# A float32 first-unit attention for the second unit too: one head per step of the first MLP

## The chip, the cores and the metric

One core of one Trainium2 chip runs the whole program. The metric is the device time of one execution in microseconds (us). Engines are named as the profile names them: PE is TensorE's matmul stream and PEld its weight loads, DVE is VectorE, ACT is ScalarE, POOL is GpSimd, SP is SyncE, whose queue issues nearly all transfers of this kernel.

## What is computed

A decayed causal attention over 4 batches, 8 heads, 576 tokens and a head size of 64 feeds an MLP with a squared ReLU, and that feeds an MLP with a leaky ReLU. Both MLPs are 512 to 2048 to 512 wide, over 2304 tokens.

```python
scores = scale * np.matmul(q, k.transpose(0, 1, 3, 2))
cum = np.cumsum(np.log(np.clip(f, 0.0001, 1.0)), axis=-1)
decay = cum[:, :, :, None] - cum[:, :, None, :]
scores = np.where(causal, -1000000000.0, scores + decay)
attn = np.exp(scores - np.max(scores, axis=-1, keepdims=True))
attn = attn / (np.sum(attn, axis=-1, keepdims=True) + 1e-09)
x = np.matmul(attn, v)                       # then heads side by side: 2304 x 512
r = np.maximum(x @ w_in, 0.0)
x = (s * (r * r) + b) @ w_out                # first MLP
h = x @ w_in2
out = np.maximum(0.01 * h, h) @ w_out2       # second MLP
```

## The kernel before

The tokens are cut into eight units (`unit_list`, L32): units 0 to 3 are the first 256 tokens of batches 0 to 3, units 4 to 7 the tokens 256 to 575. A ninth unit collects the last 64 tokens of each batch. The first MLP runs unit by unit (the loop at L816), in NF = 16 steps of 128 hidden channels. A step does `mlp1_h` (12 matmuls of L680 into one PSUM bank), `mlp1_g` on ACT, and `mlp1_o` of the step before. In unit 0 the hidden values stay float32 and `mlp1_o` is four float32 matmuls, which the trace shows as eight records of L721. In the later units it is twelve float32r matmuls (L724).

The attention of a unit must be finished when its MLP starts, so it runs beside the MLP of the unit before. There are two ways of doing it.

**The first way** (`first_a`, `first_b`, `first_c`, L529 to L601) is used for unit 0 alone, ahead of any MLP. For each head `first_a` makes scores of two query tiles (128 and 256 keys) with float32 matmuls (L540), adds the decay with a float32r matmul (L541) and the mask with a bfloat16 one (L542). DVE takes the maximum (L543, L547), and ACT the exponential with its sum (L551). `first_b` has two small DVE instructions for the reciprocal (L564, L565), scales the rows on POOL (L569), transposes three 128x128 blocks on PE (L578) and copies them out of PSUM on ACT (L580). `first_c` multiplies with V in float32 (L589) and splits the result into a high and a low float32r part (L598 on ACT, L599 on DVE). The three parts of a head run in three successive rounds.

**The second way** works in slots, one tile of queries of a head per slot. For the units 1 to 3 a head is one slot, so each has eight. A slot splits K and Q into two float32r parts (`split_head`: POOL L244, L245, DVE L246, L247) and V into two float16 parts (`split_v`: DVE L265 to L278, POOL L274, L277, and a transposing DMA, L283). `st_score` makes scores with float32r matmuls (L308) and a mask (L317), adds the decay row and takes the minimum in one DVE instruction (L320), and takes the exponential on ACT (L336). `st_split` normalizes into two float16 parts (DVE L346, L347, L358, ACT L357) and transposes them by a DMA (L362). `st_av` multiplies with V (L379) and collects (ACT L398, L413, DVE L399, L414). Loads of Q and K (`qk_raw`, L212), of V (L215) and of decay rows (`cumk`, L229) go through SP's queue.

**Weights.** The first MLP's weights come as 32 blocks of 64-bit floats (512 KB each, L89 and L94). `float_w` turns one into float32 with one ACT (L102) and three DVE instructions (L103, L104, L106); `split_w` makes the two float32r parts of a block (ACT L111, POOL L112). Step i of unit 0 needs the blocks 2i and 2i+1. Before the first MLP ten blocks are floated, the rest in unit 0's loop (L832 to L836). The output blocks get their split in unit 1 (`split_late_to`). Pool `wp` has 33 buffers (L72); Q and K of unit 0, V, the identity and the decay rows lie in it too. The tag `tt` has four buffers, shared by scores, exponentials and the temporary of `float_w`.

**Order.** A list scheduler arranges the instructions of each engine by a priority, which is the order of the program less the offset of `ahead(n)`: slots have 150, weights -100 (they fill what is left), the first way 0. `slots_to(slot_target(u, i))` says how many slots are emitted by step i of unit u. In unit 0's loop that grows from 1 to 11: unit 1's eight heads and the first three of unit 2.

Of the kernel before, what the change touches and what calls it, by code (L numbers as in the profile page):

```python
# [18 lines left out]
NQ = 384  # L19
UN = 256  # L20
QT = [(0, 128), (128, 128), (256, 128), (384, 128), (512, 64)]
PSCALE = 2.0**14
# [17 lines left out]
def attention_moe_moe_kernel(  # L40
# [124 lines left out]

    heads = [(u, h) for u in range(1, NU - 1) for h in range(H)]

# [261 lines left out]
    def ahead(n):  # L429
        return tc.high_priority(offset=n)  # L430
# [5 lines left out]
    W_BACK = 3  # L436
    W_AHEAD = 1
    LEAD = 1
# [30 lines left out]
    nc.scalar.preload_act_table_set("natural_log_exp_and_others")  # L469
    for r in range(ND // 2):  # L470
# [12 lines left out]

    cl = wp.tile([P, 2 * DM], F32R, tag="w", name="cum_hl")
    for a in range(P // BH):
        nc.gpsimd.tensor_scalar(
            cl[a * BH : (a + 1) * BH, S : S + H],
            ident[a * BH : (a + 1) * BH, a * BH : a * BH + H],
            -INV,
            0.0,  # L490
            ALU.mult,
            ALU.add,
        )
# [12 lines left out]
    for e in range(2):  # L506
# [11 lines left out]
    nc.vector.tensor_tensor_scan(cum, f_sb, f_sb, 0.0, ALU.add, ALU.bypass)  # L518
    nc.scalar.copy(cl[:BH, :S], cum)
    nc.vector.tensor_tensor(  # L520
        out=cl[BH : 2 * BH, :S], in0=cum, in1=cl[:BH, :S].bitcast(F32), op=ALU.subtract
    )
# [4 lines left out]
    e_0, sm_0, pt_0 = {}, {}, {}  # L527
    xs[0] = xp.tile([P, 2, ND, UN], F32R, tag="x", name="x", bufs=2)
    def first_a(h):  # L529
        rows = slice(h % 2 * D, (h % 2 + 1) * D)  # L530
        qt = qk_0[h // 4][rows, h // 2 % 2]
        ps = ps_o.tile([P, 512], F32, tag=f"o{h % 2}", name="ps_s0")
        e = e_0[h] = ap.tile([P, S], F32, tag="tt", name="e_0", bufs=4)
        sm = sm_0[h] = ap.tile([P, 5 * NT0], F32, tag="sm_0", name="sm_0", bufs=3)
        neg = cl[rows, S + h : S + h + 1]
        at = 0
# [45 lines left out]
    def first_c(h):  # L582
        pt = pt_0.pop(h)
        av = ps_h.tile([P, 512], F32, tag="h", name="av_0")
        pr, own = h // 2, slice(h % 2 * D, (h % 2 + 1) * D)
        at = 0
        for k in range(NT0):
            n = un0 - k * P
            nc.tensor.matmul(  # L589
                av[:, k * P : un0],  # L590
                v_0[:, k, pr * P : (pr + 1) * P],
                pt[:, at : at + n],
                start=(k == 0),
                stop=(k == NT0 - 1),
            )
            at += n
        x = xs[0]
        nc.scalar.copy(x[own, 0, pr, :un0], av[own, :un0])  # L598
        nc.vector.tensor_tensor(  # L599
            out=x[own, 1, pr, :un0], in0=av[own, :un0], in1=x[own, 0, pr, :un0].bitcast(F32), op=ALU.subtract  # L600
        )  # L601

    for h in range(H + 2):
        with ahead(P_F):
            if h >= 2:
                first_c(h - 2)
            if 1 <= h <= H:
                first_b(h - 1)
            if h < H:
                first_a(h)  # L610
# [12 lines left out]
        if h == 7:  # L623
            load_cumk(1)

# [190 lines left out]
    for u in range(NU):  # L816
# [9 lines left out]
        for i in range(NF):  # L826
# [112 lines left out]
```

## Time and profile before

| | |
|---|---|
| time, median of 3 runs | 1087.61 us (1086.0 to 1089.47) |
| the profiled execution | 1090.52 us, of which the profile's span is 1088.7 us |
| PE busy over the span | 1013.7 us (93%) |
| DVE busy | 609.9 us (56%) |
| ACT busy | 525.9 us (48%) |
| POOL busy | 242.0 us (22%) |
| first unit's attention alone | 9.4 to about 48 us |
| first unit's MLP, beside unit 1's attention | about 50 to 142 us |
| second unit's MLP, beside unit 2's attention | 142 to 222 us |

A busy share is a mean over stages that have different limits, so the profile is read by stage. Matmul records overlap (one starts before the one ahead of it ends), so the pace of PE is read from start times, not from durations. DVE records overlap a little too.

### The profile page before, as it was taken

Reading aid. Unit: us, or ns where it says so; the run is one execution under the profiler, and the core shown is the slowest. Engines: PE = TensorE matmul, PEld = TensorE weight load, DVE = VectorE, ACT = ScalarE, POOL = GpSimd, SP = SyncE. Lnnn points to the kernel's source line nnn. Section 1 sums busy time; section 2 is a strip of 40 time slices with the busy share of each in tenths; the row PEclk is TensorE's granted clock in tenths of the full one; section 3 lists DMA queues with packets and bytes.
Section 4 is the critical chain, followed back from the end, with each engine's and each line's share of the span. In section 5 each row is a group of like instructions: output and inputs, shape, how many; then the busy total and the mean of one; then the engine's idle time right before and its main releaser. Section 6 shows DMA issues by size and latency. Waiting matters only on the chain.

```text
span 1088.7 us, 18609 instructions
## 1 busy us (share of the span) xinstructions
PE 1013.7 (93%) x6728; PEld 885.8 (81%) x6728; DVE 609.9 (56%) x1522; ACT 525.9 (48%) x1283; POOL 242.0 (22%) x346
## 2 busy tenths in 40 slices
PE   7887889899899899888999999999999999999998
PEld 4676688798788788888899999777888888888887
DVE  6889988676687787777754158984311311211121
ACT  4566677565566565666664356653222222222122
POOL 5344455522122322222200014542000000000000
PEclk9999899999999999999899999999999999999999
DMA  8488465568788978889842065540200100010010
GB/s 278 159 190 242 127 150 115 132 158 165 149 191 187 199 169 190 198 175 204 190 89 78 1 208 180 174 155 0 78 1 1 59 1 1 1 39 1 1 39 20
DMA packets 188333, 127.74 MB, mean 117 GB/s; under 512 B 137488, under 2 KB 163600, under 8 KB 188240
## 3 DMA queue, kind: packets, MB, share of 16 engines
q1 hardware_dynamic: 188240, 126.54, 47.0%
q8 instruction: 53, 0.87, 0.3%
q14 instruction: 40, 0.33, 0.1%
HBM read 85.01 MB, written 10.04 MB: 87 GB/s over the span
## 4 chain that ended last, share of the span: by engine, by line
PE 48%; DMA 19%; DVE 16%; issue 7%; POOL 4%; ACT 3%; SPq 2%; POOLq 0%; DVEq 0%; ACTq 0%
PE ps_o L798 16%; PE ps_h L782 15%; DMA p_t<-p_hl 10%; PE ps_o L724 7%; PE ps_h L680 6%; DMA qk_raw<-in_qk 4%; POOL w L112 2%; DVE wt L104 2%; DMA cumk<-cumd 2%; DVE p_hl L358 2%; DVE tt L320 2%; DVE k_st L247 1%; PE ps_v L379 1%; DVE wt L106 1%; PE ps_s L540 1%
## 5 line engine op out<-in xcount | busy, mean ns | idle before, releaser
L680 PE MATMUL ps_h<-x,w 128*128 128x256 f32 x1728 | 248.9, 288 | 5.1 <-POOL w L112 3.1
L724 PE MATMUL ps_o<-g,w 128*128 128x256 f32 (+1 forms) x1536 | 233.7, 294 | 11.5 <-DVE g L705 5.4
L680 PEld LDWEIGHTS ps_h<-x,w 128*128 128x128 f32 x1728 | 224.6, 193 | 7.4 <-POOL w L112 3.6
L724 PEld LDWEIGHTS ps_o<-g,w 128*128 128x128 f32 x1536 | 203.9, 194 | 19.5 <-DVE g L705 9.9
L798 PE MATMUL ps_o<-w,g 128*128 128x512 f32 x864 | 216.1, 396 | 1.8 <-DVE g L790 1.8
L782 PE MATMUL ps_h<-x,w 128*128 128x512 f32 (+1 forms) x960 | 213.6, 370 | 0.0
L782 PEld LDWEIGHTS ps_h<-x,w 128*128 128x128 f32 x960 | 169.0, 188 | 34.3
L790 DVE TENSOR_TENSOR g<-ps_h,g 128x512 fp32r<-128x512 f32 (+1 forms) x80 | 51.0, 637 | 258.3 <-ACT g L789 258.2
L798 PEld LDWEIGHTS ps_o<-w,g 128*128 128x128 f32 x864 | 160.4, 188 | 41.6 <-DVE g L790 3.5
L788 ACT ACTIVATE ps_h<-ps_h 128x512 f32<-128x512 f32 (+1 forms) x80 | 43.1, 539 | 250.7 <-PE ps_h L782 250.7
L357 ACT ACTIVATE p_hl<-tt,sm 128x512 f16<-128x512 f32 (+4 forms) x128 | 73.7, 597 | 83.3 <-DMA p_t<-p_hl 76.5
L358 DVE SCALAR_TENSOR_TENSOR p_hl<-tt,sm,p_hl 128x512 f16<-128x512 f32 (+4 forms) x128 | 86.6, 688 | 46.3 <-ACT p_hl L357 45.5
L336 ACT ACTIVATE tt<-tt,sm 128x512 f32<-128x512 f32 (+4 forms) x128 | 76.8, 600 | 55.3 <-DVE sm L320 50.4
L308 PE MATMUL ps_s<-k_st,q_st 128*128 128x288 f32 (+4 forms) x352 | 84.5, 341 | 10.7 <-DVE sm L320 3.3
L112 POOL TENSOR_TENSOR w<-wt,w 128x512 fp32r<-128x512 f32 x48 | 69.7, 1454 | 90.0 <-ACT w L111 86.7
L379 PE MATMUL ps_v<-p_t,v_st 128*128 128x128 f16 (+1 forms) x912 | 62.0, 213 | 29.6 <-DMA p_t<-p_hl 24.3
L705 DVE TENSOR_TENSOR g<-ps_h,g 128x256 fp32r<-128x256 f32 x128 | 53.3, 418 | 48.1 <-ACT g L704 46.4
L379 PEld LDWEIGHTS <-v_st 128*128 128x128 f16 x912 | 46.8, 99 | 38.4 <-issue 18.0
L320 DVE CUSTOM_DVE_ANT_0 tt<-ps_s,cumk 128x512 f32<-128x512 f32 (+4 forms) x128 | 63.2, 495 | 12.9 <-DMA cumk<-cumd 9.7
L308 PEld LDWEIGHTS ps_s<-k_st,q_st 128*128 128x128 f32 x352 | 55.9, 195 | 15.1 <-POOL q_st L245 4.3
L702 ACT ACTIVATE ps_h<-ps_h 128x256 f32<-128x256 f32 x128 | 47.0, 367 | 37.0 <-PE ps_h L680 36.3
L245 POOL TENSOR_TENSOR q_st<-qk_raw,q_st 64x384 fp32r<-64x384 f32 (+1 forms) x56 | 58.0, 1038 | 4.3
(92 smaller groups left out, 1054.6 us busy)
## 6 DMA issues: line engine op xcount, KB each, us to landing
w_raw<-in_moe_w_in SPq DMA_DIRECT2D x32, 512.0 KB, 5.5
w_raw<-in_moe_w_out SPq DMA_DIRECT2D x32, 512.0 KB, 5.9
qk_raw<-in_qk SPq DMA_DIRECT2D x32, 480.0 KB, 4.4
cumk<-cumd SPq DMA_DIRECT2D x32, 256.0 KB, 4.3
qk_raw<-in_qk SPq DMA_DIRECT2D x24, 256.0 KB, 3.6
x1d<-x1o SPq DMA_DIRECT2D x36, 128.0 KB, 2.3
cumk<-cumd SPq DMA_DIRECT2D x32, 144.0 KB, 3.4
v_raw<-in_v SPq DMA_DIRECT2D x16, 288.0 KB, 3.4
```

The lines of the kernel that those rows point to most:

```text
L112: nc.gpsimd.tensor_tensor(w[:, 1], x, w[:, 0].bitcast(F32), ALU.subtract)
L245: nc.gpsimd.tensor_tensor(qs[D:, :qn], qr[D:], qs[D:, :qn].bitcast(F32), ALU.subtract)
L308: nc.tensor.matmul(o, q_st[j + e][:, q0 - u0 : q0 - u0 + P], k_st[j + e][:, a, k0 : k0 + kw], start=(e == 0 and a == 0), stop=(not end and ...
L320: nc.vector.tensor_tensor_reduce(tt[:, at + k0 : at + k0 + kw], o, cumk[jb][:, k0 : k0 + kw], scale=-SCALE, scalar=3.0e38 if c == 0 else s ...
L336: nc.scalar.activation(e, e, AF.Exp, bias=sm[:, r : r + 1], scale=-1.0, accum_out=sm[:, 2 + r : 3 + r])
L357: nc.scalar.mul(v[:, 0, :w], e, inv)
L358: nc.vector.scalar_tensor_tensor(v[:, 1, :w], e, inv, v[:, 0, :w], ALU.mult, ALU.subtract)
L379: nc.tensor.matmul(av[:, at + e * m : at + (e + 1) * m], v_st[j + e][:, k].rearrange("p l d -> p (l d)"), pt[:, to + l * nk + k, e * m : ( ...
L680: nc.tensor.matmul(ps, wi[:, a, d * P : (d + 1) * P], x[:, c, d], start=(d == 0 and n == 0), stop=(d == ND - 1 and n == 2),)
L724: nc.tensor.matmul(po[d], wo[:, a, d * P : (d + 1) * P], g[:, c], start=(first and n == 0), stop=(last and n == 2),)
L782: nc.tensor.matmul(ps[:, :n], wi[:, a, d * P : (d + 1) * P], x[:, e, d, :n], start=(d == 0 and k == 0), stop=(d == ND - 1 and k == 2),)
L798: nc.tensor.matmul(po[m], g[:, a, m * P : (m + 1) * P], wo[:, e, :], start=(i == 0 and k == 0), stop=(i == NF - 1 and k == 2),)
```

## The change

The first way is used for unit 1 as well (`NP = 2`). Its eight heads are spread over the steps of unit 0's MLP: step i does `first_c` of head i-2, `first_b` of head i-1 and `first_a` of head i. In steps 0 to 7 no slot is emitted; from step 8 on the three slots of unit 2 follow. The slots and the transposing DMAs of unit 1 are gone. Q, K and V of unit 1 are loaded in the first way's layout, in rounds 5 and 6 of unit 0's attention. The identity and the decay rows get buffers of their own outside `wp`. Unit 1's scores and products use the PSUM banks of the slots. The first loads for slots (`load_heads`, `load_cumk`, `split_head(0)`) move from unit 0's attention to the steps 5 and 6 of its MLP, and they are now those of unit 2. The weights of unit 0's loop are asked for and floated further ahead: at step i, 4i+16 blocks loaded and 3i+12 floated, where it was 2i+8 and 2i+3.

```diff
-    heads = [(u, h) for u in range(1, NU - 1) for h in range(H)]
+    heads = [(u, h) for u in range(NP, NU - 1) for h in range(H)]
...
+    def load_first(r):
+        qk_0.append(wp.tile([P, 2, 2 * un0], F32, tag="w", name="qk_0"))
         for e in range(2):
             nc.sync.dma_start(out=qk_0[r][:, e], in_=qk0[2 * r + e])
-        if r == 0:
-            for _ in range(W_FIRST):
-                w1.load(nc.sync)
-            v_0 = wp.tile([P, NT0, DM], F32, tag="w", name="v_0")
-            nc.sync.dma_start(out=v_0, in_=v0.rearrange("(k p) c -> p k c", p=P))
-    misc = wp.tile([P, 2 * DM], F32, tag="w", name="misc")
-    ident = misc[:, :P]
+        if r % (ND // 2) == 0:
+            if r == 0:
+                for _ in range(W_FIRST):
+                    w1.load(nc.sync)
+            v_0.append(wp.tile([P, NT0, DM], F32, tag="w", name="v_0"))
+            nc.sync.dma_start(out=v_0[-1], in_=v0[r // (ND // 2)].rearrange("(k p) c -> p k c", p=P))
+
+    for r in range(ND // 2):
+        load_first(r)
+    ident = const.tile([P, P], F32, name="ident")
     make_identity(nc, ident)
-    cl = wp.tile([P, 2 * DM], F32R, tag="w", name="cum_hl")
+    cl = const.tile([P, un0 + NP * H], F32R, name="cum_hl")
...
-        ps = ps_o.tile([P, 512], F32, tag=f"o{h % 2}", name="ps_s0")
+        if h < H:
+            ps = ps_o.tile([P, 512], F32, tag=f"o{h % 2}", name="ps_s0")
+        else:
+            ps = ps_a.tile([P, 512], F32, tag="ps_s", name="ps_s0", bufs=3)
...
-        av = ps_h.tile([P, 512], F32, tag="h", name="av_0")
+        if h < H:
+            av = ps_h.tile([P, 512], F32, tag="h", name="av_0")
+        else:
+            av = ps_a.tile([P, 512], F32, tag="ps_v", name="av_0")
...
+    def first_step(b, i):
+        with ahead(P_F):
+            if 2 <= i < H + 2:
+                first_c(b * H + i - 2)
+            if 1 <= i <= H:
+                first_b(b * H + i - 1)
+            if i < H:
+                first_a(b * H + i)
+
     for h in range(H + 2):
...
+        first_step(0, h)
+        if h in (5, 6):
+            load_first(h - 3)
...
-        if h == 6:
-            load_heads()
-            load_cumk(0)
-            split_head(0)
-        if h == 7:
-            load_cumk(1)
...
     def slot_target(u, i):
+        if u < NP - 1 and i < 8:
+            return 0
...
             if u == 0:
-                while len(w1.blocks) < min(2 * NF, 2 * i + 8):
+                while len(w1.blocks) < min(2 * NF, 4 * i + 16):
                     w1.load(nc.sync)
                 with ahead(P_W):
-                    w1.split_to(2 * i + 2 + W_AHEAD)
+                    w1.split_to(3 * i + 12)
...
+            if u < NP - 1:
+                first_step(u + 1, i)
+                if i == 5:
+                    load_heads()
+                    load_cumk(0)
+                    split_head(0)
+                if i == 6:
+                    load_cumk(1)
```

## Rows read from the trace of the kernel before

**Rows 1.** Page, slices: busy tenths of 40 equal slices of the span

```profile
PE   7887889899899899888999999999999999999998
DVE  6889988676687787777754158984311311211121
```

**Rows 2.** By stage: us, then PE, PEld, DVE, ACT, POOL busy, PEclk, DMA share, GB/s

```profile
9.40:44.00 34.60, 33.00 (x103) 22.69 (x103) 26.33 (x71) 19.00 (x57) 15.90 (x23) 1.00 0.85 285
44.00:50.00 6.00, 5.10 (x28) 4.28 (x27) 5.94 (x14) 3.05 (x9) 1.59 (x2) 1.00 0.00 0
50.00:142.00 92.00, 74.97 (x466) 65.37 (x466) 86.41 (x227) 58.90 (x154) 44.99 (x49) 0.93 0.68 175
142.00:222.00 80.00, 70.16 (x561) 65.28 (x559) 62.40 (x189) 55.38 (x163) 42.93 (x51) 0.96 0.58 136
```

**Rows 3.** DVE by line, 50 to 142 us: busy us, mean ns, idle before

```profile
L104 DVE SCALAR_TENSOR_TENSOR wt<-w_raw,wt 128x512 int32<-128x512 int32 x23 | 19.8, 861 | 0.0
L358 DVE SCALAR_TENSOR_TENSOR p_hl<-tt,sm,p_hl 128x256 f16<-128x256 f32 (+1 forms) x22 | 10.6, 505 | 0.4 <-ACT p_hl L357 0.3
...
L106 DVE SCALAR_TENSOR_TENSOR wt<-w_raw,wt 128x512 int32<-128x512 int32 x11 | 8.1, 738 | 0.0
...
L269 DVE TENSOR_SCALAR vs<-vs 128x1 int32<-128x1 int32 x6 | 0.8, 139 | 0.0
```

**Rows 4.** DVE by line and shape, 9 to 44 us: first way, first and last of six

```profile
L543 DVE TENSOR_REDUCE sm<-ps_s 128x1 f32<-128x256 f32 x8 | 3.4, 422 | 3.7 <-PE ps_s L542 3.5
...
L565 DVE RECIPROCAL sm<-sm 128x2 f32<-128x2 f32 x8 | 1.3, 160 | 0.0
```

**Rows 5.** PE in order of time: start us, us, engine, line, operation, count

```profile
23.89 0.79 PE L540 MATMUL ps_s<-qk 64*128 64x128 f32 x2
...
24.95 1.22 PE L540 MATMUL ps_s<-qk 64*128 64x256 f32 x2
...
26.39 0.85 PE L578 MATMUL ps_t<-misc,e 128*128 128x128 f32 x3
...
29.04 2.77 PE L589 MATMUL av<-pt,v 128*128 128x256 f32 x8
31.80 0.79 PE L540 MATMUL ps_s<-qk 64*128 64x128 f32 x2
...
48.01 0.92 PE L589 MATMUL av<-pt,v 128*128 128x256 f32 x4 [0.90 <-ACT pt L580]
48.68 1.31 PE L680 MATMUL ps_h<-x,w 128*128 128x256 f32 x9
...
51.50 3.32 PE L680 MATMUL ps_h<-x,w 128*128 128x256 f32 x26 [0.68 <-DVE x L599]
54.66 1.89 PE L721 MATMUL ps_o<-g,w_raw 128*128 128x256 f32 x8
56.20 1.29 PE L680 MATMUL ps_h<-x,w 128*128 128x256 f32 x8
```

**Rows 6.** PE by line, 50 to 142 us: largest and smallest of a slot's three matmuls

```profile
L308 PE MATMUL ps_s<-k_st,q_st 128*128 128x128 f32 (+1 forms) x48 | 12.9, 339 | 3.9 <-DVE k_st L246 1.7 <-DVE k_st L247 1.6 <-DVE sm L320 0.4
...
L379 PE MATMUL ps_v<-p_t,v_st 128*128 128x128 f16 x59 | 5.3, 228 | 5.5 <-DMA p_t<-p_hl 3.3 <-DVE x_raw L399 1.9
```

**Rows 7.** Waits of SP's queue, 0 to 145 us: total, times, longest

```profile
SPq L229 <- DVE sm L320: 32.0, 7, 19.1
```

**Rows 8.** Stretches of 5 us in the first MLP, columns as in rows 2

```profile
95.00:100.00 5.00, 2.64 (x17) 2.26 (x15) 4.97 (x14) 3.25 (x7) 2.63 (x3) 0.86 0.84 242
110.00:115.00 5.00, 3.37 (x23) 2.72 (x22) 5.00 (x12) 2.42 (x6) 3.04 (x3) 1.00 0.49 106
115.00:120.00 5.00, 4.07 (x21) 3.52 (x19) 5.00 (x16) 3.96 (x11) 2.20 (x4) 0.57 0.86 263
```

More of the change, by code (lines that the diff above doesn't have):

```diff
@@ L20 @@
 UN = 256
+NP = 2
 QT = [(0, 128), (128, 128), (256, 128), (384, 128), (512, 64)]
@@ L436, in attention_moe_moe_kernel @@
     W_BACK = 3
-    W_AHEAD = 1
     LEAD = 1
@@ L469, in attention_moe_moe_kernel @@
     nc.scalar.preload_act_table_set("natural_log_exp_and_others")
-    for r in range(ND // 2):
+    v_0 = []
+    def load_first(r):
         qk_0.append(wp.tile([P, 2, 2 * un0], F32, tag="w", name="qk_0"))
@@ L518, in attention_moe_moe_kernel @@
     nc.vector.tensor_tensor_scan(cum, f_sb, f_sb, 0.0, ALU.add, ALU.bypass)
-    nc.scalar.copy(cl[:BH, :S], cum)
+    nc.scalar.copy(cl[:BH, :un0], cum[:, :un0])
     nc.vector.tensor_tensor(
-        out=cl[BH : 2 * BH, :S], in0=cum, in1=cl[:BH, :S].bitcast(F32), op=ALU.subtract
+        out=cl[BH : 2 * BH, :un0], in0=cum[:, :un0], in1=cl[:BH, :un0].bitcast(F32), op=ALU.subtract
     )
@@ L527, in attention_moe_moe_kernel @@
     e_0, sm_0, pt_0 = {}, {}, {}
-    xs[0] = xp.tile([P, 2, ND, UN], F32R, tag="x", name="x", bufs=2)
+    for u in range(NP):
+        xs[u] = xp.tile([P, 2, ND, UN], F32R, tag="x", name="x", bufs=2)
     def first_a(h):
@@ L531, in first_a @@
         qt = qk_0[h // 4][rows, h // 2 % 2]
-        ps = ps_o.tile([P, 512], F32, tag=f"o{h % 2}", name="ps_s0")
+        if h < H:
+            ps = ps_o.tile([P, 512], F32, tag=f"o{h % 2}", name="ps_s0")
+        else:
+            ps = ps_a.tile([P, 512], F32, tag="ps_s", name="ps_s0", bufs=3)
         e = e_0[h] = ap.tile([P, S], F32, tag="tt", name="e_0", bufs=4)
         sm = sm_0[h] = ap.tile([P, 5 * NT0], F32, tag="sm_0", name="sm_0", bufs=3)
-        neg = cl[rows, S + h : S + h + 1]
+        neg = cl[rows, un0 + h : un0 + h + 1]
         at = 0
@@ L583, in first_c @@
         pt = pt_0.pop(h)
-        av = ps_h.tile([P, 512], F32, tag="h", name="av_0")
-        pr, own = h // 2, slice(h % 2 * D, (h % 2 + 1) * D)
+        if h < H:
+            av = ps_h.tile([P, 512], F32, tag="h", name="av_0")
+        else:
+            av = ps_a.tile([P, 512], F32, tag="ps_v", name="av_0")
+        u, pr = h // H, h % H // 2
+        own = slice(h % 2 * D, (h % 2 + 1) * D)
         at = 0
@@ L590, in first_c @@
                 av[:, k * P : un0],
-                v_0[:, k, pr * P : (pr + 1) * P],
+                v_0[u][:, k, pr * P : (pr + 1) * P],
                 pt[:, at : at + n],
@@ L596, in first_c @@
             at += n
-        x = xs[0]
+        x = xs[u]
         nc.scalar.copy(x[own, 0, pr, :un0], av[own, :un0])
@@ L601, in first_c @@
         )
-    for h in range(H + 2):
[L604 to L610, printed above, removed]
+    def first_step(b, i):
[6 more added lines that the diff above has]
+                first_a(b * H + i)
+    for h in range(H + 2):
+        first_step(0, h)
+        if h in (5, 6):
+            load_first(h - 3)
         if h == 3:
@@ L908 @@
     host = {
-        "qk0": _np.concatenate([qT[0, :, :, :n0], kT[0, :, :, :n0]], axis=2).reshape(H // 2, 2 * D, 2 * n0),
-        "v0": inputs["v"][0, :, :n0].transpose(1, 0, 2).reshape(n0, H * D),
+        "qk0": _np.concatenate([qT[:NP, :, :, :n0], kT[:NP, :, :, :n0]], axis=3).reshape(
+            NP * H // 2, 2 * D, 2 * n0
+        ),
+        "v0": inputs["v"][:NP, :, :n0].transpose(0, 2, 1, 3).reshape(NP, n0, H * D),
         "qk": _np.concatenate(
@@ L913 @@
                 x
-                for b, u0, un, _ in unit_list(B, S)[1:]
+                for b, u0, un, _ in unit_list(B, S)[NP:]
                 for h in range(H)
```

4 lines of the change are left out of this document (2 added, 2 removed).

## The prediction

> **What bounds the kernel now.** I read the page's slices first [rows 1]. From the twentieth slice on PE stands at nine tenths or more to the end, and DVE is mostly below it. In slices three to five (54 to 136 us), inside the first unit's MLP, it is the other way round: PE at eight, seven, eight, DVE at eight, nine, nine. So there is a stage near the start whose limit is not PE, and it is the one that the change touches. The second view is the table by stage [rows 2]. The first unit's attention (9.4 to 44 us) keeps PE busy 33.0 of 34.6 us. The first unit's MLP (50 to 142 us) takes 92 us with DVE busy 86.4 of them and PE only 75.0. The second unit's MLP has the same matmuls but for the float32 output half, and takes 80 us with DVE at 62.4. So the first MLP stage is set by DVE.
>
> The third view says what DVE does there [rows 3]. Its 20 groups add up to 101.5 us of durations against 86.4 busy, since records overlap, so a duration counts 0.85. Four groups are the weights (L103, L104 and L106 twice, 48.3 us). Fourteen are the second way of attention (from L358 to L269, 52.4 us) for about eleven heads: unit 1's eight and three of unit 2. That is 4.76 us per head, 4.05 after the overlap.
>
> **DVE, part by part.** Eight heads of the second way go: 8 x 4.05 = 32.4 us less. Eight of the first way come. They have six DVE instructions each, whose means add up to 1.71 us [rows 4], 1.45 after the overlap, or 11.6 us. The weights stay. DVE's work in the stage falls from 86.4 to about 65.6 us.
>
> **PE, part by part.** PE's work must be read from start times [rows 5]. L680 does 26 in 3.16 us (51.50 to 54.66), so twelve take 1.46; eight L721 take 1.54 (54.66 to 56.20). A step of the first MLP is 3.0 us, sixteen are 48.
>
> A head of the first way I take from the first unit's attention: scores of the small tile with mask and decay 1.06 us (23.89 to 24.95), of the large one 1.44 (24.95 to 26.39), three transposes 0.85, four products with V 1.38 (eight from 29.04 to 31.80). That is 4.73 us. But PE ran slowly there: four L589 took 1.38 us at 29 us and 0.67 us at 48.01, just ahead of the first MLP matmuls. The granted-clock column reads 1.00 in both stretches [rows 2], yet the pace doubles, as between the levels 1.2 and 2.4 GHz. Beside the MLP I take the fast pace: 4.73 x 0.67/1.38 = 2.3 us per head, 18 for eight; the slow end would be 38.
>
> Three slots of unit 2 remain. The three matmul groups of slots were busy 23.9 us for eleven heads [rows 6], 2.2 per head at most; paced as the eight L721 are (1.54 us of 1.89 busy [rows 5]) it is 1.8, so I take 5 us for three. PE's work is 48 + 18 + 5 = 71 us, above DVE's 65.6. **The bound passes from DVE to PE, and the two come close.**
>
> **From work to stage.** Two things stretch the 71 us. The granted clock was 0.93 in this stage and 0.96 in the next [rows 2]; I take 0.95. PE waits: a transpose (L578) now sits in PE's queue behind POOL's scaling (L569), and the product (L589) behind ACT's copy (L580). Queued behind them are the output matmuls of the step before and the next `mlp1_h`; `mlp1_g` on ACT waits for those. The same three parts, also one round apart, with weights floated beside them, kept PE busy 95% from 9.4 to 44 us [rows 2], so I take 0.95. 71 / 0.95 / 0.95 = 78.7 us, against 92: 13.3 us less. The ends are 71 (full clock, no wait) and 71 / 0.93 / 0.88 = 87 (waits as in the second unit's MLP, 70.16 of 80).
>
> **Smaller edits.** Unit 1's first scores no longer lie between the last first-way heads and the MLP's start, where PE was busy 5.1 of 6 us and DVE 5.94 [rows 2]. I count 1 us earlier (0 to 2).
>
> The extra loads of rounds 5 and 6 are four of 256 KB and one of 512 KB, 1.5 MB or 5 us at the 285 GB/s of that stretch. They pass weight blocks on SP's queue. DMA stands at 0.00 from 44 to 50 us [rows 2], which covers them; without that cover weights come 5 us later, and the ten blocks floated before the MLP still serve five steps. I count nothing.
>
> Sixteen transposing DMAs leave SP's queue. So does a wait: `cumk` of the slots stood in it for up to 19.1 us with weight loads queued behind [rows 7]. This helps only the weights' supply: nothing counted.
>
> Weights asked for earlier meet `wp`'s 33 buffers. Three stay with Q, K and V of unit 1 until steps 3, 7 and 9, and a V load and a block being split take two, so 28 blocks fit, enough to step 13. Nothing, unless a load that waits for a buffer holds the Q and K of unit 2 behind it on SP: then POOL and DVE stand in `split_head`. The price is between 0 and 5 us, and I take 0, since the nearest wait of that kind (19.1 us) held weights and DVE was busy 5.94 of 6 us at that time. The tag `tt` now holds two exponentials much of the time and leaves two of four buffers for floating weights, as in the first unit's attention; 0 to 5 us, taken as 0 because floating is asked for five steps ahead.
>
> ACT (58.9 us) and POOL (45.0) have room in 79 us and get no more work. At the end of the stage the same three heads of unit 2 have been scored as before, so I leave all that follows (142 us to the end) unchanged.
>
> **Sum.** 13.3 + 1 = 14.3 us. The profiled execution took 1090.5 us and would take 1076.2; the median of the runs shown lies 2.9 us lower, 1087.6, which gives 1073.3.
>
> **Rivals.** (a) *PE keeps the full clock and the waits vanish, so DVE and PE overlap nearly whole:* stage 71 to 74 us, total about 1067. For it: fewer stops of PE, and the weights are fillers that can go anywhere in the stage. Against: both engines would be above 90%.
>
> (b) *The gain drowns in waits of PE's queue or in the buffers above:* stage 85 to 92 us, total 1080 to 1088. For it: the second unit's MLP takes 80 us with even less PE and DVE work. Against: there a DMA transpose lies in each slot, here not in the first eight steps.
>
> (c) *PE's clock stays at its lower level, and the kernel gets slower.* For it: from 9.4 to 44 us the first way ran at the slow pace for all 34 us, although PE was busy 95% [rows 2, 5]. In the first MLP the granted clock already falls: 0.86 in a stretch where PE was busy 2.64 of 5 us, 0.57 in the one after a stretch of 3.37 [rows 8]. Against: 26 MLP matmuls run at the fast pace right after the attention, and 3 of every 5.3 us are MLP matmuls in the new steps. Price: ten steps of 3.0 and eight heads of 2.3 are 48 us at the fast level, double at the slow. Slow for half of that work: 71 + 24 = 95 us, over 0.95 for waits 100, so 8 us more than now, about 1095; slow for all of it about 1120. It decides from about 16 us of that work on: (71 + 16) / 0.95 = 92.
>
> The page "TensorE: Matmul & The Clock Gate" of the Trainium skill (Part 4, PE-mode transpose) says that for transposes in transpose mode the full clock does not engage. By that rule the stage would tend to (c), 1095. The trace agrees in part: the three transposes of a head took 0.85 us in the slow stretch, but so slow were the ordinary float32 products beside them too [rows 5].
>
> (d) *The change does not take DVE's load off*, because floating is pulled so far ahead that it, not attention, fills DVE in the first eight steps and delays the maxima: 22 blocks at 48.3 x 0.85 / 22 = 1.9 us are 41 us, plus 11.6, in eight steps of 5.3 (42 us). Then these steps take 53 us, the other eight 32, total 85 less 92: 1080, or 1087 with waits.
>
> **How the numbers follow.** Forecast 0.53 (1069 to 1078), (a) 0.17, (b) 0.13, (c) 0.13, (d) 0.04. The range runs from 1064, the full clock without a wait (92 - 71 and 2 for the earlier start), to 1090, which takes in (b) and (d); beyond it lie most of (c) and a rest of (a). What a measurement of this kernel can tell from no change is about 0.3%, 3.3 us. Faster: forecast, (a) and nearly half of (b), 0.76. Same: the rest of (b) and (d), 0.10. Slower: (c) and a little more, 0.14.
>
> **What would show it.** In the new profile the first MLP should end near 127 us after the start, DVE should be busy about 66 us and PE's idle time should be small from the MLP's start to its end. A head's four L589 should take about 0.67 us there; 1.4 us means (c). DVE over 90% while PE waits means (b) or (d). The stages behind should be as long as before; the prediction is wrong if slots of the later units run late, or if work that PE saved is waited for again further on.

## The result, and the profile after

The change makes the kernel slower. The median is 1100.99 us (1095.98 to 1102.51) against 1087.14 us for the kernel before on the same chip, a ratio of 1.0117 [1.008, 1.0153]. The forecast was 1073.3 us, and the range ended at 1090. The profiled execution of after took 1102.51 us, with a span of 1100.7 us against 1088.7 before.

From here on L553 to L616 of after are the lines L540 to L601 of before (scores L553, transposes L591, products with V L606), L698 is `mlp1_h` (L680 before), L739 the float32 `mlp1_o` (L721). Some of the experiments have them two to six lines further on. "A unit's end" is the first instruction on ACT that scales a result of its MLP.

The page of after, first its span, then its engines and slices, the ones shown in [rows 1] for before:

```profile
span 1100.7 us, 18470 instructions
...
PE 1028.9 (93%) x6752; PEld 899.7 (82%) x6752; DVE 588.5 (53%) x1458; ACT 517.7 (47%) x1271; POOL 237.2 (22%) x338
...
PE   7898979899989899888899999999999999999998
...
DVE  6767687777776777677754139985311311211111
```

In slices three to five, inside the first MLP, DVE has fallen from 8, 9, 9 to 6, 7, 6, and PE now stands at 9, 8, 9. So the bound did pass from DVE to PE. The time by stage says that it bought nothing. Columns as in [rows 2]. The rows of after are the MLP of the first unit, of the second, and of the third to seventh together; those of before are the second unit and the third to seventh.

After:

```profile
52.00:142.30 90.30, 83.57 (x470) 71.42 (x469) 61.83 (x153) 47.73 (x130) 33.25 (x39) 0.94 0.26 70
142.30:226.00 83.70, 72.75 (x559) 67.69 (x558) 62.49 (x194) 56.74 (x168) 44.09 (x52) 0.92 0.51 130
226.00:602.70 376.70, 339.13 (x3038) 313.95 (x3037) 265.06 (x765) 224.60 (x581) 88.48 (x144) 0.98 0.80 167
```

Before:

```profile
142.00:218.00 76.00, 66.16 (x538) 61.52 (x535) 59.48 (x180) 53.00 (x157) 42.16 (x49) 0.98 0.56 132
217.80:590.10 372.30, 340.51 (x3039) 314.71 (x3038) 265.58 (x768) 226.51 (x581) 83.86 (x144) 0.98 0.79 170
```

| stage | before, us | after, us | difference | forecast |
|---|---|---|---|---|
| to the end of unit 0's MLP | 141.9 | 142.3 | +0.4 | -14.3 |
| unit 1's MLP | 75.9 | 83.7 | +7.8 | 0 |
| units 2 to 6 | 372.3 | 376.7 | +4.4 | 0 |
| the rest of the span | 498.6 | 498.0 | -0.6 | 0 |
| sum | 1088.7 | 1100.7 | +12.0 | -14.3 |

So there are two things to explain: a first stage that lost 20 us of DVE work and ended no earlier, and 12 us in stages whose work was not touched.

What the first stage does is seen on PE in order of time (columns as in [rows 5]), here from one product with V to the next head's, and then the last head. Behind it stands PE's largest wait of the stage (total, times, longest):

```profile
66.63 0.87 PE L606 MATMUL av<-pt,v 128*128 128x256 f32 x4
67.33 0.60 PE L739 MATMUL ps_o<-g,w_raw 128*128 128x256 f32 x2
...
70.03 1.78 PE L698 MATMUL ps_h<-x,w 128*128 128x256 f32 x12
71.66 0.27 PE L591 MATMUL ps_t<-ident,e 128*128 128x128 f32 x1
71.86 0.48 PE L553 MATMUL ps_s<-qk 64*128 64x128 f32 x2
...
72.40 0.39 PE L591 MATMUL ps_t<-ident,e 128*128 128x128 f32 x2
...
76.90 0.59 PE L606 MATMUL av<-pt,v 128*128 128x256 f32 x2
77.42 0.70 PE L553 MATMUL ps_s<-qk 64*128 64x256 f32 x2
...
83.75 0.27 PE L591 MATMUL ps_t<-ident,e 128*128 128x128 f32 x1
83.95 0.48 PE L553 MATMUL ps_s<-qk 64*128 64x128 f32 x2
...
129.76 0.28 PE L591 MATMUL ps_t<-ident,e 128*128 128x128 f32 x1
129.79 0.48 PE L310 MATMUL ps_s<-k_st,q_st 128*128 128x256 f32 x2
...
PE ps_t L591 <- POOL e L582: 3.0, 5, 1.3
```

The order is the same for every head: the first transpose of a head (71.66), then the small-tile scores of the next head (71.86), then its other transposes (72.40). A head's scores never stand ahead of the transposes of the head before. Those wait for the maximum, the exponential, the reciprocal and POOL's scaling of their own head, so one head is under way at a time, and there are 12 us from one first transpose to the next (71.66, 83.75). PE waits 3.0 us in all for that scaling. Matmuls of the MLP stand in PE's order too, 5.6 us from a head's small scores (71.86) to its large ones (77.42). Over all eight heads the products with V run from 66.6 to 134.4 us, 9.7 us per head. And the scores of unit 2's first slot (129.79) stand behind a transpose of the last head: the slots' first pass on DVE comes at 131.5 us, against 116.3 before.

What that does to PE is read in stretches of 5 us of after (columns as in [rows 2]):

```profile
75.00:80.00 5.00, 5.00 (x31) 4.20 (x30) 1.02 (x3) 2.07 (x8) 0.98 (x1) 1.00 0.00 0
...
100.00:105.00 5.00, 3.01 (x14) 1.95 (x13) 4.09 (x10) 3.20 (x8) 1.99 (x3) 0.94 0.17 66
105.00:110.00 5.00, 4.02 (x17) 3.19 (x16) 3.31 (x10) 2.26 (x9) 2.13 (x3) 0.50 0.00 0
110.00:115.00 5.00, 5.00 (x17) 3.99 (x17) 3.49 (x7) 1.94 (x5) 2.03 (x2) 0.54 0.02 5
```

At 75 us PE is full with MLP matmuls and DVE nearly idle. By 97 us eleven of the sixteen MLP steps have run (132 records of L698), but only four heads. Then there is little left that PE can put between the heads: it is busy 3.01 of 5 us, and in the ten microseconds behind that the granted clock is at the lower of its two levels (0.50, 0.54).

### The profile page after: what moved, and what is told of

It is laid out like the page before. It is cut to its first block, busy times and chain, and to the rows that moved or that the text cites. A ratio compares the mean times of both kernels' runs of the same rounds, so it can differ in the third digit from the quotient of the medians.

```text
span 1100.7 us, 18470 instructions
## 1 busy us (share of the span) xinstructions
PE 1028.9 (93%) x6752; PEld 899.7 (82%) x6752; DVE 588.5 (53%) x1458; ACT 517.7 (47%) x1271; POOL 237.2 (22%) x338
## 4 chain that ended last, share of the span: by engine, by line
PE 57%; DMA 16%; DVE 10%; issue 6%; POOL 4%; ACT 4%; SPq 2%; POOLq 0%; DVEq 0%; ACTq 0%
PE ps_o L816 16%; PE ps_h L800 15%; PE ps_h L698 10%; PE ps_o L742 9%; DMA p_t<-p_hl 8%; POOL w L114 3%; PE ps_o L739 2%; PE ps_v L381 2%; DMA qk_raw<-in_qk 2%; PE ps_s L310 2%; DVE p_hl L360 1%; DMA cumk<-cumd 1%; PE ps_s L553 1%; DVE wt L106 1%; DMA v_st<-v_hl 1%
## 5 line engine op out<-in xcount | busy, mean ns | idle before, releaser
L698 PE MATMUL ps_h<-x,w 128*128 128x256 f32 x1728 | 254.0, 292 | 3.2 <-POOL w L114 2.0
L698 PEld LDWEIGHTS ps_h<-x,w 128*128 128x128 f32 x1728 | 229.9, 196 | 4.5 <-POOL w L114 2.4
L800 PEld LDWEIGHTS ps_h<-x,w 128*128 128x128 f32 x960 | 169.4, 189 | 32.8
L359 ACT ACTIVATE p_hl<-tt,sm 128x256 f16<-128x256 f32 (+3 forms) x112 | 67.4, 619 | 78.7 <-DMA p_t<-p_hl 76.0
L360 DVE SCALAR_TENSOR_TENSOR p_hl<-tt,sm,p_hl 128x256 f16<-128x256 f32 (+3 forms) x112 | 76.8, 696 | 42.9 <-ACT p_hl L359 42.2
L338 ACT ACTIVATE tt<-tt,sm 128x512 f32<-128x512 f32 (+4 forms) x112 | 69.5, 621 | 45.6 <-DVE sm L322 45.1
L310 PE MATMUL ps_s<-k_st,q_st 128*128 128x288 f32 (+4 forms) x320 | 74.2, 342 | 12.1 <-DVE sm L322 7.6
L322 DVE CUSTOM_DVE_ANT_0 tt<-ps_s,cumk 128x512 f32<-128x512 f32 (+4 forms) x112 | 57.3, 517 | 12.0 <-DMA cumk<-cumd 9.4
L310 PEld LDWEIGHTS ps_s<-k_st,q_st 128*128 128x128 f32 x320 | 50.0, 195 | 15.0 <-DVE sm L322 7.0
L246 POOL TENSOR_SCALAR q_st<-qk_raw 128x384 fp32r<-128x384 f32 (+1 forms) x48 | 28.8, 601 | 122.5 <-DMA qk_raw<-in_qk 83.1
```

Of the source, the lines that this page charges most:

```text
L310: nc.tensor.matmul(o, q_st[j + e][:, q0 - u0 : q0 - u0 + P], k_st[j + e][:, a, k0 : k0 + kw], start=(e == 0 and a == 0), stop=(not end and ...
L322: nc.vector.tensor_tensor_reduce(tt[:, at + k0 : at + k0 + kw], o, cumk[jb][:, k0 : k0 + kw], scale=-SCALE, scalar=3.0e38 if c == 0 else s ...
L338: nc.scalar.activation(e, e, AF.Exp, bias=sm[:, r : r + 1], scale=-1.0, accum_out=sm[:, 2 + r : 3 + r])
L359: nc.scalar.mul(v[:, 0, :w], e, inv)
L360: nc.vector.scalar_tensor_tensor(v[:, 1, :w], e, inv, v[:, 0, :w], ALU.mult, ALU.subtract)
L698: nc.tensor.matmul(ps, wi[:, a, d * P : (d + 1) * P], x[:, c, d], start=(d == 0 and n == 0), stop=(d == ND - 1 and n == 2),)
```

## The experiments

The theory after the two traces: **banks and order**. In unit 0 the scores have a PSUM tag of their own (`ps_o`). In unit 1 scores, transposes and the slots' scores take the three banks of one tag (`ps_s`) in turn, and the program asks for the transposes of head i-1 before the scores of head i. The rivals: the exponentials hold the `tt` buffers (**buffers**), weights asked for earlier take DVE and `wp` (**pace**), and a mere rearrangement by the list scheduler (**order by chance**).

One table for all of them, from the traces. "Passes" counts how many score passes of the slots of unit 2 and later DVE has done (two per slot) when unit 0's MLP ends; at the end of unit 1's MLP it is 34 in every kernel. "First output" is the start of the first `mlp1_o` on PE, and the last column counts from there to the end of unit 1's MLP. Each ratio is to runs of before made beside that kernel, whose medians were 1087.1 us for after, 1089.2 for e1 to e4, 1087.6 for e5 to e8 and 1089.4 for e9 and e10. The stages are those of one profiled execution each.

| kernel | median us | ratio to before | end of unit 0 | passes | unit 1's MLP | its end | units 2 to 6 | first output | from it to the end of unit 1 |
|---|---|---|---|---|---|---|---|---|---|
| before | 1087.1 | | 141.9 | 8 | 75.9 | 217.8 | 372.3 | 54.7 | 163.1 |
| after | 1101.0 | 1.0117 [1.008, 1.0153] | 142.3 | 7 | 83.7 | 226.0 | 376.7 | 57.8 | 168.2 |
| e1 | 1084.9 | 0.9973 [0.9952, 0.9995] | 142.9 | 8 | 72.4 | 215.3 | 369.1 | 54.5 | 160.9 |
| e2 | 1091.5 | 1.0018 [0.9997, 1.0038] | 137.9 | 7 | 83.4 | 221.3 | 371.0 | 53.2 | 168.1 |
| e3 | 1097.2 | 1.0071 [1.0047, 1.0095] | 131.9 | 3 | 88.9 | 220.8 | 370.9 | 52.3 | 168.5 |
| e4 | 1080.6 | 0.9928 [0.9904, 0.9953] | 130.8 | 8 | 70.2 | 201.0 | 381.2 | 58.7 | 142.2 |
| e5 | 1089.2 | 1.0006 [0.9987, 1.0026] | 124.3 | 6 | 82.6 | 206.9 | 379.6 | 59.4 | 147.5 |
| e6 | 1107.1 | 1.0163 [1.0131, 1.0194] | 165.9 | 12 | 68.3 | 234.2 | 375.2 | 56.1 | 178.1 |
| e7 | 1106.0 | 1.0154 [1.013, 1.0178] | 121.5 | 0 | 108.6 | 230.1 | 376.8 | 52.7 | 177.4 |
| e8 | 1074.5 | 0.9873 [0.9854, 0.9891] | 131.3 | 8 | 68.6 | 199.9 | 374.0 | 59.0 | 140.9 |
| e9 | 1081.8 | 0.9926 [0.9903, 0.995] | 123.3 | 2 | 79.5 | 202.8 | 381.2 | 55.2 | 147.7 |
| e10 | 1088.4 | 0.9989 [0.9969, 1.0009] | 128.3 | 6 | 79.7 | 208.0 | 376.6 | 55.5 | 152.5 |

The last column is there because "first output" differs between kernels whose order is the same up to it. In e2 every engine has its instructions in the order of after until the end of unit 1's MLP, and yet its first MLP ends 4.4 us earlier. All of that lies ahead of the first output (53.16 us against 57.79); from there to the end of unit 1's MLP both take 168 us. Likewise the +0.4 us of the first stage is a later start and a shorter run: from the first output to the end of its MLP unit 0 took 87.2 us before and 84.5 after. The last section shows what differs there. So an end of the first MLP may be off by some 5 us from one execution to another.

**The pace of the weights (e6, e7).** e6 is the change with the old pace of loading and floating, e7 the kernel before with the new pace alone.

```
e6:  -   while len(w1.blocks) < min(2 * NF, 4 * i + 16):
     +   while len(w1.blocks) < min(2 * NF, 2 * i + 8):
     -       w1.split_to(3 * i + 12)
     +       w1.split_to(2 * i + 3)
e7:  the same two lines of before, the other way round
```

> The changed kernel with the weights' old pace (2i+8 loaded, 2i+3 floated at step i). In PE's order the heads then stand closer together and ahead of the last six steps of the MLP, and the slots of unit 2 start among those steps. Theory stream: the eighth score pass starts well before 140 us, at 115 to 132, and the span is that plus 948, 1063 to 1080, even if the first MLP ends at 140 us or later. Theory stage: span is the end of the first MLP plus 948, so 1088 or more for an end at 140. If the pace was what delayed the heads, the heads follow each other in 5 to 8 us here.

> The kernel before with nothing but the weights' new pace (4i+16 loaded, 3i+12 floated). The rest of the change is left out. If the pace alone does the harm: the slots of unit 1 and 2 come later than before, the first MLP ends after 145 us and the total is 1092 or more. If it only harms together with heads in turn: 1080 to 1092, the spread that a new order of the later stages brings.

e6, two stretches of the first MLP (columns as in [rows 2]), and the longest wait of SP's queue in it (total, times, longest):

```profile
52.00:100.00 48.00, 41.65 (x212) 33.35 (x210) 18.18 (x58) 18.90 (x56) 10.94 (x17) 0.86 0.01 2
100.00:130.00 30.00, 22.67 (x114) 18.45 (x113) 24.84 (x61) 17.09 (x46) 15.44 (x15) 0.85 0.54 154
...
SPq L285 <- DVE wt L106: 56.7, 1, 56.7
```

From 52 to 100 us there is no DMA (share 0.01): a transposing DMA of `split_v` stands in SP's queue for 56.7 us, and the weight loads are behind it. Only seven of the sixteen MLP steps have run by 100 us, and the first MLP ends at 165.9 us. So the change needs its new pace. But the pace does bear on the heads: with fewer MLP matmuls between them, they follow each other in 7.5 us (ACT's copies of their results run from 66.3 to 118.5 us) where in after it is 10.1, with the banks and the order of asking as in after. That lies in the 5 to 8 us named above for "the pace delayed the heads". The slots' eighth pass, expected at 115 to 132 us, came at 155.1.

e7, first and second MLP:

```profile
52.00:121.50 69.50, 61.09 (x377) 53.93 (x375) 67.16 (x155) 43.06 (x110) 33.83 (x32) 0.98 0.63 173
121.50:230.10 108.60, 83.68 (x606) 76.78 (x605) 75.27 (x242) 65.77 (x196) 49.18 (x62) 0.84 0.51 122
```

The pace alone, without the new heads, makes the first MLP end 20 us earlier, and the kernel 1.5% slower. None of unit 2's slots has begun by then, and unit 1's own last score pass comes only at 123.0 us. The first twelve matmuls of its MLP in a row start at 143.5. Unit 1's MLP takes 108.6 us. So a gain in the first MLP can be given back, and more, in the second. How much of the 108.6 us is this late start and how much the clock (0.84 granted) no run settles.

**Buffers (e3).** The exponentials of unit 1 go to another tag, so that they hold none of the four `tt` buffers.

```
     -   e = e_0[h] = ap.tile([P, S], F32, tag="tt", name="e_0", bufs=4)
     +   e = e_0[h] = (ap.tile([P, S], F32, tag="tt", name="e_0", bufs=4) if h < H
     +                 else ap.tile([P, 5 * P], F32, tag="p_hl", name="e_0"))
```

> The changed kernel, with the exponentials of unit 1's heads in the slots' p_hl buffers, so that the four tt buffers are left to the floating of weights. Its order from the second unit's MLP on is that of the kernel before on all engines (2393 of 2898 rows of PE). Theory order: the time behind the first stage is that of before, 448 us between the ends of the first and the seventh unit, and the total is 1087 plus or minus 4. Theory backlog: 455 us or more. If the tt buffers hold the heads back in the first stage, that stage ends 5 us or more before 142; if not, at 139 to 145.

```profile
52.00:131.90 79.90, 72.57 (x421) 62.30 (x420) 52.99 (x122) 41.96 (x110) 29.99 (x32) 0.96 0.21 65
131.90:220.80 88.90, 74.90 (x578) 68.88 (x578) 65.70 (x214) 59.38 (x181) 47.09 (x57) 0.91 0.58 132
```

The first MLP ends 10.4 us earlier than in after, but 5.5 of these lie ahead of the first output (52.3 against 57.8 us), where the order on PE is the same, and only three passes are done instead of seven. The slots still start late (first pass at 129.1 us). From the first output to the end of unit 1's MLP, where the passes are equal, e3 takes 168.5 us and after 168.2: that the buffers hold anything back is not shown. Between the ends of the first and the seventh unit lie 459.8 us, on the side of "backlog", and all of it is unit 1's MLP (88.9): units 2 to 6 take 370.9, where before takes 372.3, and on every engine the records of the two stand in the same order from about 210 us on. The profiled execution of e3 lies 6 us below its median.

**Order and banks (e4, e5).** e4 emits the scores of head i ahead of the transposes of head i-1; nothing else differs. e5 leaves the order and gives the transposes banks of another tag (`ps_v`).

```
e4, in first_step:
     +       if b and i < H:
     +           first_a(b * H + i)
             if 1 <= i <= H:
                 first_b(b * H + i - 1)
     -       if i < H:
     +       if not b and i < H:
                 first_a(b * H + i)
e5, in first_b:
     -   ps = ps_a.tile([P, 512], F32, tag="ps_s", name="ps_t0", bufs=3)
     +   ps = (ps_a.tile([P, 512], F32, tag="ps_s", name="ps_t0", bufs=3) if h < H
     +         else ps_a.tile([P, 512], F32, tag="ps_v", name="ps_t0"))
```

> The changed kernel with the scores of head i emitted ahead of the transposes of head i-1 in each step. Both take PSUM banks of one tag, and in the changed kernel's order a head's scores never stand ahead of the transposes of the head before. If that is what lets only one head be under way (theory: banks in turn), the heads follow each other in 6 to 8 us in place of 11, and the first MLP ends at 128 to 136 us. If the heads' pace comes from somewhere else, it ends at 139 to 145. The later order differs from both kernels, so the total says little: theory order allows 1075 to 1105.

> The changed kernel with the transposes of unit 1's heads in the bank of the products with V (ps_v), so that scores no longer share a tag with them. Two theories of what sets the total. Theory stream: the slots of unit 2 can only start behind the last head's scores, and from then on the slots of all units take their time; in the runs so far the span is the start of unit 2's eighth score pass plus 948 us (942 to 956). Here the slots stand among the last heads in PE's order, so the eighth pass should start at 120 to 132 us and the span be 1068 to 1082. Theory stage: what counts is the end of the first unit's MLP, as in the prediction; span is that end plus 948 (946 to 958).

e4, first and second MLP, and PE in order of time:

```profile
52.00:130.80 78.80, 78.12 (x482) 68.15 (x481) 64.96 (x160) 50.73 (x138) 36.86 (x42) 0.99 0.30 89
130.80:201.00 70.20, 61.63 (x512) 57.37 (x511) 57.28 (x180) 51.73 (x158) 38.18 (x46) 1.00 0.60 135
```

```profile
70.32 0.89 PE L606 MATMUL av<-pt,v 128*128 128x256 f32 x4
...
72.88 0.70 PE L553 MATMUL ps_s<-qk 64*128 64x256 f32 x2
...
73.69 0.28 PE L591 MATMUL ps_t<-ident,e 128*128 128x128 f32 x1
74.01 0.48 PE L553 MATMUL ps_s<-qk 64*128 64x128 f32 x2
...
74.43 0.44 PE L591 MATMUL ps_t<-ident,e 128*128 128x128 f32 x2
...
78.81 0.81 PE L606 MATMUL av<-pt,v 128*128 128x256 f32 x4
```

Now both score tiles of the next head stand ahead of (72.88) or between (74.01) the transposes. ACT's copies of the eight heads' results run from 68.7 to 120.0 us, 7.3 us per head, where in after they run from 67.5 to 138.0, 10.1 per head. The slots start at 116.2 us, as before. The stage takes 78.8 us against 90.3. The two rows show where its 11.5 us come from, as an estimate: PE's idle time is 0.7 us instead of 6.7 (6.0 us), and the share of the clock that was not granted is 0.01 of 78.8 instead of 0.06 of 90.3 (0.8 instead of 5.4, 4.6 us). Unit 1's MLP follows with 70.2 us against 83.7. At its end e4 is 25 us ahead of after and 17 ahead of before. In e5 the first MLP ends at 124.3 us, with PE busy all of the time. But its heads are hardly faster than in after: their results come from 65.5 to 129.5 us, 9.1 us per head, the last one behind the end of the first MLP. What comes earlier is the slots' first pass, at 112.8 us against 131.5. So the two edits act on different parts: e4 lets the heads follow each other faster, e5 takes the slots' scores out of the heads' turn. From the first output to the end of unit 1's MLP, after takes 168.2 us, e4 142.2 and e5 147.5. That the shared banks and the order of asking for them hold the two first stages is thereby shown. That they alone set the pace of the heads is not, since in e6 the heads took 7.5 us with both as in after; the MLP matmuls that stand between the heads are the other part.

But the totals are 1080.6 and 1089.2 us, less of a gain than 17 and 11 us at the end of unit 1's MLP: units 2 to 6 take 381.2 and 379.6 us, where before took 372.3 with the same work. Both sums of 948 us fail in e5: its eighth pass comes at 126.6 us and its first MLP ends at 124.3, which gives 1074.6 and 1072.3 us, and the span was 1084.6.

**Order by chance (e1, e2).** The scheduler arranges all that follows anew after any edit. A neutral one measures what that is worth: the slots' priority is 151 instead of 150, in e1 for the kernel before, from slot 11 on, in e2 for the kernel after, from slot 3 on (the same heads).

```
     -   with ahead(P_ATT):
     +   with ahead(P_ATT if slot_no < 11 else 151):     (e2: < 3)
```

> The kernel before, with the slots' priority at 151 in place of 150 from slot 11 on; all of it up to the end of the first unit's MLP stands in the same order, and what comes later is arranged anew. If the order in which the scheduler happens to set the later stages is worth several us (theory: order), the time from the end of the first MLP unit to that of the seventh moves from 448 us by 3 to 15 us either way, with the same work. If the loss of the changed kernel comes from what its first stage leaves behind (theory: backlog), this edit does nothing: 448 us plus or minus 2, total 1087 plus or minus 3.

> The changed kernel with the same edit (priority 151 from slot 3 on). Its first stage stands as in the changed kernel, and from the third unit's MLP on its instructions stand on every engine in the same order as in the kernel before with 151. Theory order: the two then differ only in the first two stages, total within 4 us of the kernel before with 151. Theory backlog: it stays 10 to 14 us slower than the kernel before with 151.

One step of priority moves the kernel after by 1.0% (ratios 1.0117 and 1.0018), and before by 0.3% (0.9973). In e1 the time between the ends of the first and the seventh unit moves from 448.2 us to 441.6, as the theory of order has it. e2 has the same order as e1 on every engine behind its early part (in the traces, the last 5291 of 6752 records of PE, from 261 us on in e2), so this pair compares the change with what follows held equal: 1091.5 against 1084.9 us, 6.6 us slower instead of 13.9, which neither theory had named. At the end of unit 1's MLP they are 6.0 us apart (221.3, 215.3), and the units 2 to 6 differ by 1.9; from the first output to the end of unit 1's MLP it is 168.1 us against 160.9. The second pair of equal order, before and e3, differs there by 1.4. So the loss in units 2 to 6 is rearrangement; the loss ahead of them is the change's own.

**Together (e8, e9, e10).** e8 is e4 with the priority of e2. e9 is e8 with unit 2's first three slots emitted only behind unit 0's MLP. e10 is e8 with the buffers of e3.

```
e9:  -   if u < NP - 1 and i < 8:
     +   if u < NP - 1:
             return 0
     -   with ahead(P_ATT if slot_no < 3 else 151):
     +   with ahead(0 if slot_no < 3 else 151):
```

> The changed kernel with the scores of head i ahead of the transposes of head i-1, as in the run before it that had this edit, and the slots' priority at 151 from slot 3 on. The first stage stands in the same order, the later ones in another. Theory order: the first MLP ends at 131 us as there, and the rest moves by 3 to 12 us either way from its 950 us.

> The fastest version so far (scores ahead of transposes, slot priority 151), with the first three slots of unit 2 emitted only behind the first unit's MLP and at priority 0. Nothing else is changed in the first stage, so the heads of unit 1 and the first MLP end as they did, at 127 to 132 us. Theory stream: fewer score passes of unit 2 are done by then (2 to 4 in place of 8), the second unit's MLP takes 80 to 90 us in place of 69, its end moves from 200 to 209 us or later, and the total from 1074.5 to 1082 or more. Theory stage: the second unit's MLP keeps 69 to 73 us and the total stays at 1069 to 1080, within what a new order of the later stages does.

> The fastest version so far with the exponentials of unit 1's heads in the slots' p_hl buffers as well. If the tt buffers still hold back the heads or the floating once scores go first, the first MLP ends at 121 to 127 us in place of 131 and the total is 1064 to 1072, as far as the slots of unit 2 start earlier too. If not, it ends at 128 to 134 us and the total is 1069 to 1082.

e8, by stage, and the engines of its page:

```profile
52.00:131.30 79.30, 78.62 (x485) 68.65 (x485) 65.45 (x160) 50.77 (x139) 36.89 (x42) 1.00 0.28 86
131.30:199.90 68.60, 61.40 (x516) 57.37 (x516) 58.69 (x180) 51.72 (x156) 38.52 (x46) 1.00 0.56 142
199.90:573.90 374.00, 343.93 (x3067) 315.98 (x3066) 264.01 (x771) 226.66 (x584) 87.75 (x146) 0.99 0.82 170
```

```profile
PE 1018.3 (95%) x6752; PEld 888.1 (83%) x6752; DVE 587.7 (55%) x1458; ACT 517.5 (48%) x1271; POOL 234.0 (22%) x338
```

e8 takes 1074.5 us (1073.4 to 1075.9), 1.3% less than before and 2.4% less than the change as it was made: **this version beats both**. It shares the order of the later units with e1 and e2, from about 300 us on, and its median is 10.4 us below that of e1. Its span is 16.8 us under that of before: 10.6 in unit 0's MLP, 7.3 in unit 1's, 0.6 at the end, less 1.7 in units 2 to 6.

e9 asks whether the first MLP's length may be judged alone. Without the three slots it ends 8.0 us earlier than in e8, 3.9 of them ahead of the first output, where the order is the same. Unit 1's MLP then takes 10.9 us more, and ends 2.9 later. Counted from the first output, e9 is 4.1 us earlier at the first of these ends and 6.8 later at the second (147.7 against 140.9). A shorter first stage was bought by work that the second had to do: the view that the first MLP's end is what counts falls, and the view that the slots' stream is what counts is right in direction, though the second MLP ended at 202.8 us and not at 209 or later. (Units 2 to 6, 381.2 us against 374.0, make up the rest of e9's loss; their order differs, and no run holds it equal.)

e10 misses: with the scores first, buffers of their own bring the first MLP's end only from 131.3 to 128.3, and even that lies ahead of the first output (55.5 against 59.0 us), where the order on PE is the same. Unit 1's MLP takes 11.1 us more, from six passes instead of eight. What puts its slots behind is not settled; their first pass is no later than in e8 (115.0 against 116.6 us). Its profiled execution (1084.3 us) also lies 4 us below its median.

## Why the prediction was wrong

**DVE's work: right.** 61.8 us in the stage, where 65.6 was forecast, and the bound passed to PE.

**PE's work: right for a head, too small in sum.** Four products with V take 0.70 us beside the MLP (66.63 to 67.33), as the step from the slow to the fast pace had it. With the scores first, the stage takes 78.8 us from 52 us on, 80.8 from 50, near the forecast length (78.7). That is luck: PE is busy 78.1 of the 78.8 at a clock of 0.99, so its work is about 77 us, not 71, and the factors for waits and clock were hardly needed. Twelve L698 in a row take 1.63 us (70.03 to 71.66) where 1.46 was counted. Of the 216 matmuls of `mlp1_h` in e4's stage only 192 are unit 0's, so two steps of unit 1's MLP have begun. And the eight passes are four slots, where three were counted, in before as well.

**One microsecond of earlier start: wrong.** The first MLP's matmuls start at 49.21 us (48.68 before [rows 5]), with a large score tile of unit 1 among them, and still at the slow pace (last section). The first output comes at 57.79 us against 54.66, 3.1 us later. In e2, with the same order, it came at 53.16, so this part differs from one execution to another.

**From work to stage: this step failed.** I took the share of 0.95 from the first unit's attention, because "the same three parts, also one round apart" kept PE busy 95% there. They are the same three parts, but in unit 0 the scores have banks of their own; in unit 1 they take banks in turn with the transposes and with unit 2's slots. I looked at `tt` and `wp` and not at the PSUM tags, although the tag is in the diff (`ps_s` for `h >= H`). The upper end of the stage, 87 us, was passed: it took 90.3 from 52 us on, 92.3 from 50 as the forecast counts, with 6.7 us of idle PE and 5.4 us of clock. With about 77 us of work, as in e4, and the slow pace at the start, that roughly makes up the length. This is rival (b) in its place, a wait of PE's queue, and nearly in its length (85 to 92 us). But the sign I named for it, DVE over 90% while PE waits, did not come: DVE was busy 68% and PE 93%. A chain that passes through several engines need not fill any of them.

**The stages behind: this step failed too, and it has more of the loss against before.** I left them unchanged because "at the end of the stage the same three heads of unit 2 have been scored as before". In before it was four heads (8 passes), and in after nearly as many (7 passes), yet unit 1's MLP took 7.8 us more. The table shows what I should have priced: by the end of unit 1's MLP each kernel has done 34 passes, so the heads of unit 1, the first 17 slots and two MLPs are one stage with two exits. Kernels with 12 or 8 passes at the first exit take 68 to 76 us to the second, those with 7 or fewer 79.5 to 108.6. The count orders them only roughly (6 passes 79.7 and 82.6, 7 passes 83.7, 2 passes 79.5), so it is a mark of how late the slots' stream is rather than a price. Of the 7.8 us some 5 are clock, as an estimate: 0.08 of 83.7 us not granted (6.7) against 0.02 of 76.0 (1.5). Why the clock falls there in after, and not in e4, is open.

**Rival (c), the clock, was not the cause.** At 0.94 the stage's clock is about that of before (0.93 [rows 2]), the low stretch follows a stretch in which PE was busy 3.01 of 5 us, and e4 runs the same heads at 0.99. It came as a price on the waits. What it did cost by itself is the slow pace that reached into the first MLP (last section). The Trainium skill's page "TensorE: Matmul & The Clock Gate" (Part 4, PE-mode transpose), by which the full clock does not engage for such transposes, is not borne out here as far as their own pace goes: two L591 take 0.39 us at 72.40 in after, and two took 0.64 in the slow stretch at 46.23 (its row is in the last section).

**Rival (d) was wrong**: DVE had room in the stage (busy 61.8 of 90.3 us, and 1.02 of 5 at 75 us). **Rival (a)** (71 to 74 us) is nearly reached in length by e5 (72.3 from 52 us on, 74.3 from 50), but not with its other half: e5's unit 1 takes 82.6 us.

**The loss in units 2 to 6** (4.4 us) no step of the prediction allowed for. Over the twelve kernels these units took 369 to 381 us with the same work. About 6 us either way belongs to a forecast for this kernel, and the range should have had it.

## What to carry to other kernels

When a pipeline is moved beside another, list for each of its stages the tag its tiles come from and who else takes from that tag, in the order in which the program asks: tiles of one tag are handed out in that order, and here it paid that the next item's first stage asked before the last item's late stage. Price coupled stages up to the first point where the program forces the same state (here 34 passes at the end of the second MLP), since a gain at an earlier mark can be work put off, or an earlier start that differs from one execution to the next. Where a list scheduler orders the rest, hold that order equal in both kernels, or measure a neutral edit, before a difference of half a per cent is read as an effect.

## What the runs showed of the hardware that was not expected

The granted-clock column is no sign of the pace early in the run. PE of after around the start of the first MLP:

```profile
46.23 0.64 PE L591 MATMUL ps_t<-ident,e 128*128 128x128 f32 x2
47.91 1.65 PE L606 MATMUL av<-pt,v 128*128 128x256 f32 x4 [1.04 <-ACT pt L593]
49.21 2.27 PE L698 MATMUL ps_h<-x,w 128*128 128x256 f32 x9
...
52.82 5.14 PE L698 MATMUL ps_h<-x,w 128*128 128x256 f32 x27
57.79 0.38 PE L739 MATMUL ps_o<-g,w_raw 128*128 128x256 f32 x1
```

In e4 and e8 the first unit's attention and the start of the first MLP stand in the same order. From 44 to 50 us (columns as in [rows 2], e4 first) PE does the same in the same time, and the column reads 0.50 in one and 1.00 in the other:

```profile
44.00:50.00 6.00, 5.84 (x20) 3.94 (x19) 5.97 (x12) 3.48 (x7) 1.61 (x2) 0.50 1.07 378
44.00:50.00 6.00, 5.84 (x20) 3.93 (x20) 5.94 (x12) 3.45 (x8) 1.58 (x3) 1.00 1.06 378
```

So the slow pace is the lower level of the clock, and the 1.00 of e8 in this stretch does not tell it, nor that of after, whose four L606 took 1.44 us like e4's (from 43.53 to 44.97, and from 43.29 to 44.73). The column reads 1.00 at 47.9 us in after, where four L606 took 1.30 us (47.91 to 49.21), and the same four took 0.70 at 66.63. The slow pace went over into the first MLP: 27 L698 took 4.97 us from 52.82 (to 57.79), where 26 had taken 3.16 before [rows 5]. In e2, whose order is that of after, the column reads 0.61 from 44 to 50 us and 1.00 from 50 to 55, and its 27 matmuls at the same place took 3.60 us:

```profile
49.56 3.76 PE L698 MATMUL ps_h<-x,w 128*128 128x256 f32 x27
53.16 1.89 PE L739 MATMUL ps_o<-g,w_raw 128*128 128x256 f32 x8
```

So how long the slow pace lasts differs between executions of the same order, and it is worth several microseconds at the first MLP's start. The twelve kernels also show how far a fall of the clock can be the effect of a wait: in after the ten microseconds at half the clock stand right behind a stretch in which PE was busy 60% of the time, and with the waits gone (e4, e8) the stage ran at 0.99 to 1.00.
